# Turning batch 1's dilated q and k by DMA instead of on TensorE, and a new order at the start of an output stage

## The chip, the cores and the metric

The kernel runs on one core of one Trainium2 chip. The core has five engines with instruction queues of their own: TensorE (PE in the profile; its weight loads are PEld), VectorE (DVE), ScalarE (ACT), GpSimd (POOL) and SyncE (SP, which here only issues transfers). Sixteen DMA engines move data between the chip's memory and the core's on-chip memory (SBUF); TensorE writes its results to PSUM, eight banks of 128 x 512 float32. Each engine takes its instructions strictly in program order, so one that waits holds up all that stand behind it. The metric is the device time in microseconds (us).

## The reference: what is computed

Attention with two kinds of masks, then a gated feed-forward block on its result. Cut to what matters:

```python
batch, n_heads, seq, head_dim = (8, 8, 576, 64)          # q, k, v, float32
scores = scale * np.matmul(q, k.transpose(0, 1, 3, 2))
mask_plain = (rel >= 0) & (rel < 32)                     # heads 0-3
mask_dil = (rel >= 0) & (rel < 128) & (rel % 4 == 0)     # heads 4-7
attn = softmax over the positions that the mask leaves
x = (attn @ v), heads side by side                       # 4608 tokens x 512
g, val = x @ w_gate, x @ w_val                           # 512 x 1536 each
out = (gelu(g) * val) @ w_out                            # 1536 x 512
```

A dilated head sees only keys that are a multiple of four positions away, so its 576 positions fall into four classes of 144 that never meet. In scores and values the kernel handles a class as 128 + 16 positions.

## The kernel before: the parts that matter here

The 4,608 tokens are nine chunks of 512, c = 0 to 8. A chunk has a first feed-forward part (`ffn1`, twelve blocks `nb` of gate and value products with GELU) and an output stage (`ffn2`, four blocks `tb` of 128 tokens, each a chain of twelve matmuls over `u_all` and `wo`). The attention of the batches whose tokens come next is woven into the output stages. A batch has four units of work, two plain pairs of heads and two dilated ones; n = 4 to 7 are those of batch 1 (4 and 5 plain, 6 and 7 dilated). For each unit: scores on TensorE (`emit_s`, `s_of`), an exponential on ScalarE, a multiplication by the mask on VectorE (`mask_next`), the sums of the rows on TensorE (`den`), their reciprocals on VectorE (a 32x32 transpose, a reciprocal, a transpose back), the weighted values on TensorE (`num`) and a multiplication on VectorE that writes `xT`.

Scores need q and k with the head dimension on the partitions, so they must be transposed. For the dilated heads of batches 0 and 1 TensorE does this, from a tile that holds eight positions of a head per partition (72 partitions):

```python
    def load_eights(b):
        q8 = ldp.tile([R8, 2, HK, 8, D], F16, tag="qd", name=f"qd{b}")     # R8 = 72
        for t, src in ((0, q), (1, k)):
            tiles["last"] = nc.gpsimd.dma_start(
                out=q8[:, t].rearrange("p h r d -> p h (r d)"), in_=eights(src, b, HK, H)
            )
        return q8

    def t_dil(b, hp, q8, b0, engs):
        qtd_ = tiles["qT", b][1]
        for t in range(2):
            for hl in range(2):
                for r in range(4):
                    ...
                    nc.tensor.transpose(ps16[:, b0 + t, c0 : c0 + R8], ..., ident[0:R8, 0:R8])
            copy(engs[t], qtd_[:, t, 2 * hp : 2 * hp + 2]..., ps16[:, b0 + t, 0:S]...)
```

Batches 2 to 7 load four positions per partition, 128 partitions and a rest of 16, and let the DMA engines transpose. Transfers issued from GpSimd turn float32 into float16 on the way:

```python
    def load_qk_dil(b):
        qd = ldp.tile([P, 2, HK, 4, D], F16, tag="qd", name=f"qd{b}")
        rd = ldp.tile([16, 2, HK, 4, D], F16, tag="rd", name=f"rd{b}")
        for t, src in ((0, q), (1, k)):
            nc.gpsimd.dma_start(out=fl(qd[:, t]), in_=quads(src, b, HK, 0, 4 * P))
        for t, src in ((0, q), (1, k)):
            nc.gpsimd.dma_start(out=fl(rd[:, t]), in_=quads(src, b, HK, 4 * P, S))
        return qd, rd
```

`last_keys` copies the last 64 columns of every key class from `qTd` to `kTr`, which the dilated scores read as well:

```python
    def last_keys(b, h0, h1, eng=nc.vector):
        _, qtd_, ktr = tiles["qT", b]
        eng.tensor_copy(ktr[:, h0:h1], qtd_[:, 1, h0:h1, :, NCL - 64 : NCL])
```

The loads of batch 1, in program order (a `gate` makes a transfer wait until another one has landed):

```python
    load_w(2)                                   # POOL: wg, wv
    gate["dma"] = w1
    st1 = ldp.tile([R6, 2, HK, 6 * D], F32, tag="st", name="st1")
    for t, src in ((0, q), (1, k)):
        gated(nc.sync.dma_start(out=st1[:, t], in_=sixes(src, 1)))      # SP: plain q, k
    sv1 = new_v(1)
    new_qt(1)
    qd1 = load_eights(1)                        # POOL: dilated q, k
    wo1 = [load_wo(i) for i in range(3)][1]     # POOL: wo0, wo1, wo2
    load_v_dil(1)                               # POOL: vd, vr, vr
    q61 = ldp.tile([R6, 2, 6, HK, D], F16, tag="qp", name="qp1")
    for hp in range(2):
        for t in range(2):
            cast_six("pool", q61, st1, t, hp)   # POOL: four casts to float16
    gate["dma"] = wo1
    v_plain(1, sv1, nc.sync)                    # SP: plain v
    v_cast(1, sv1)
    tiles["plain", 2] = load_batch_plain(2)
```

In blocks 10 and 11 of the first feed-forward part TensorE transposes the plain q and k that those casts made:

```python
            if c == 0 and nb > 9:
                t_plain(1, q61, nb - 10, (4, 2)[nb - 10], ("act", "dve"))
```

Then comes the output stage of chunk 0, in which `third(tb, i)` is four of the twelve matmuls of block `tb`, on bank `tb`:

```python
            s_of(4)
            t_dil(1, 0, qd1, 0, ("dve", "dve"))
            t_dil(1, 1, qd1, 2, ("act", "dve"))
            mask_next()
            last_keys(1, 0, HK)
            third(0, 0)
            s_of(5)
            third(1, 0)
            mask_next()
            den(4, 0)
            s_of(6)
            third(0, 1)
            mask_next()
            third(1, 1)
            den(5, 0)
            s_of(7)
            third(0, 2)
            mask_next()
            den(6, 0)
            third(1, 2)
            ffn2(c, 2, 0, {3: [lambda: num(4, 4)], 8: [lambda: den(7, 0)]})
            store(c, 2, 0, "act")
            ffn2(c, 3, 1, {2: [lambda: num(5, 6)]})
            store(c, 3, 1, "act")
            num(6, 2)
            num(7, 4)
            gelu_table()
```

Of the kernel before, what the change touches and what calls it, by code (L numbers as in the profile page):

```python
# [21 lines left out]
def kernel(  # L22
# [10 lines left out]
    nc = tc.nc  # L33
# [3 lines left out]
    P = 128  # L37
    NHP = H // 2
    HK = H // 2
    NCL = S // DIL  # L40
# [117 lines left out]
    tiles = {}  # L158
# [82 lines left out]
    def load_eights(b):  # L241
        q8 = ldp.tile([R8, 2, HK, 8, D], F16, tag="qd", name=f"qd{b}")
# [5 lines that stand above are left out]
# [5 lines left out]
    def load_v_dil_rest(b):  # L253
        for m in range(2):
# [2 lines left out]
                in_=quads(v, b, HK, S - 256, S)[:, :, 2 * m * D : 2 * m * D + 2 * D],  # L257
            )

    def load_batch_plain(b):  # L260
        st = load_qk_plain(b)
        sv = new_v(b)
        v_plain(b, sv, nc.sync)
        return st, sv
# [5 lines left out]
    def load_batch_rest(b):  # L270
        st, sv = tiles["plain", b]
        qd, rd = load_qk_dil(b)
        qp = cast_qk_plain(b, st)
        load_v_dil(b)
        v_cast(b, sv)
        new_qt(b)
        qtp_, qtd_, _ = tiles["qT", b]
        dst = qtd_.rearrange("p t h m i -> p (t h m) i")
        nc.sync.dma_start_transpose(out=dst[:, :, 0:P], in_=qd.rearrange("p t h r d -> p (t h r d)"))
        nc.sync.dma_start_transpose(out=dst[:, :, P:NCL], in_=rd.rearrange("p t h r d -> p (t h r d)"))  # L280
        dst = qtp_.rearrange("p t h c -> p (t h) c")
        for kb in range(5):
            n = min(P, S - kb * P)
            nc.sync.dma_start_transpose(
                out=dst[:, :, kb * P : kb * P + n], in_=qp[0:n, kb].rearrange("p t h d -> p (t h d)")
            )
        last_keys(b, 0, HK, nc.gpsimd)
# [17 lines left out]
    def cast_six(eng, q6, st, t, hp):  # L305

        h = slice(2 * hp, 2 * hp + 2)
        copy(eng, q6[:, t, :, h, :], st[:, t, h, :].rearrange("p h (r d) -> p r h d", r=6))
# [305 lines left out]
    def ffn2(c, tb, bank, hooks=None, fcs=range(NNB)):  # L614
        for fc in fcs:
            for hook in (hooks or {}).get(fc, ()):
                hook()
            nc.tensor.matmul(  # L618
                ps[:, bank, :],
                u_all[:, fc, tb * P : (tb + 1) * P],  # L620
                wo_t[fc // 4][:, fc % 4, :],
                start=(fc == 0),
                stop=(fc == NNB - 1),
            )
# [69 lines left out]
    def den(n, b0, dt=None):  # L694
        emit_pv(n, b0, ("den",), wide=True)
        return norm_r(n, b0, wide=True, dt=dt)

    def num(n, b0):
        emit_pv(n, b0, ("num",))
        norm_x(n, b0)  # L700
# [35 lines left out]
        gated(nc.sync.dma_start(out=st1[:, t], in_=sixes(src, 1)))  # L736
    sv1 = new_v(1)
    new_qt(1)
    qd1 = load_eights(1)
    wo1 = [load_wo(i) for i in range(3)][1]  # L740
    load_v_dil(1)
    q61 = ldp.tile([R6, 2, 6, HK, D], F16, tag="qp", name="qp1")
    for hp in range(2):
        for t in range(2):
            cast_six("pool", q61, st1, t, hp)
    gate["dma"] = wo1
    v_plain(1, sv1, nc.sync)
    v_cast(1, sv1)
# [21 lines left out]
    for c in range(NCH):  # L770
        if 1 <= c and c + 2 < B:
            tiles["plain", c + 2] = load_batch_plain(c + 2)
            load_batch_rest(c + 2)
        pv_at = values_a.get(c, {})
        s_list = list(scores.get(c, ()))
        if c < 2:
            pairs = ((2, 3), (0, 1))
        else:
            pairs = (ends, (mm0 + 1, mm0 + 2))
        SB = 4 - mm0  # L780

        masks = []
        pend = None
        for nb in range(NNB):
            if nb == 0 and c < 2:
                ffn1_two(c, ((4, 5), (6, 7)) if c == 0 else ((6, 7), (0, 1)), range(NKC), False)
            elif nb == 0 and late:
                ffn1_two(c, pairs, (2, 3, 0, 1) if c in (2, 3) else range(NKC), True)
            elif nb > 1 or not (c < 2 or late):
                ffn1(c, nb, pairs[nb % 2])  # L790
            if pend is not None:
                (norm_both_x if is_plain(pend) else norm_x)(pend, SB)
                pend = None
            if nb in pv_at:
                pend = pv_at[nb]
                if is_plain(pend):
                    emit_both(pend, SB)
                    norm_both_r(pend, SB)
                else:
                    emit_pv(pend, SB, wide=True)  # L800
                    norm_r(pend, SB, wide=True)
            if c == 0 and nb > 9:
                t_plain(1, q61, nb - 10, (4, 2)[nb - 10], ("act", "dve"))
            if nb == NNB - 1 and c > 0 and s_list:
                n = s_list.pop(0)
                masks.append(emit_s(n, SB, pe_mask=n in biased))

        def s_next():
            if s_list:
                n = s_list.pop(0)  # L810
                masks.append(emit_s(n, SB, pe_mask=n in biased))

        def mask_next():
            mask = masks.pop(0) if masks else None
            if mask is not None:
                mask()


        if c == 0:
            load_batch_rest(2)  # L820

            def third(tb, i):
                ffn2(c, tb, tb, fcs=range(4 * i, 4 * i + 4))
                if i == 2:
                    store(c, tb, tb, "act")

            def s_of(n):
                masks.append(emit_s(n, 4))


            s_of(4)
            t_dil(1, 0, qd1, 0, ("dve", "dve"))
            t_dil(1, 1, qd1, 2, ("act", "dve"))
            mask_next()
            last_keys(1, 0, HK)
            third(0, 0)
            s_of(5)
            third(1, 0)
            mask_next()
            den(4, 0)  # L840
            s_of(6)
            third(0, 1)
            mask_next()
            third(1, 1)
            den(5, 0)
            s_of(7)
            third(0, 2)
            mask_next()
            den(6, 0)
            third(1, 2)  # L850
            ffn2(c, 2, 0, {3: [lambda: num(4, 4)], 8: [lambda: den(7, 0)]})
            store(c, 2, 0, "act")
            ffn2(c, 3, 1, {2: [lambda: num(5, 6)]})
            store(c, 3, 1, "act")
# [3 lines that stand above are left out]
        else:  # L858
            todo = list(values_b.get(c, ()))
            lone = c in values_b  # L860

            ends = (3, 0) if c == 1 else ends
            going = []

            def do(kind, tb):
                if kind == "s":
                    s_next()
                elif kind == "m":
                    mask_next()
                elif kind == "x":  # L870
                    norm_x(*going.pop(0))
                elif kind == "v":
                    n, flip = todo.pop(0), ends[tb % 2] != mm0
                    bank = mm0 + 1 - flip
                    emit_pv(n, bank, flip=flip)
                    norm_r(n, bank, flip=flip)
                    going.append((n, bank, flip))
                else:
                    n = todo.pop(0)
                    emit_pv(n, SB)  # L880
                    norm_parts(n, SB, min(S, (c + 2) * CH - n // NHP * S))

            for tb in range(4):
                at = [(fc, kind) for t, fc, kind in places.get(c, ()) if t == tb]
                hooks = {}
                for fc, kind in at:
                    if fc < NNB:
                        hooks.setdefault(fc, []).append(lambda kind=kind, tb=tb: do(kind, tb))
                bank = ends[tb % 2] if lone else mm0 + tb
                if c == NCH - 1 and tb == 3:  # L890
                    last_block(c, tb, bank)
                    break
                ffn2(c, tb, bank, hooks)
                store(c, tb, bank, "dve" if c > 5 and tb == 3 else "act")
                for fc, kind in at:
                    if fc == NNB:
                        do(kind, tb)
            if lone:
                gelu_table()

            late = lone and len(values_b[c]) > 2
            if c == 3:
                mm0 = 4 - mm0
            if c == 3 or not lone:
                ends = (mm0, mm0 + 3)
            while masks:
                mask_next()
# [28 lines left out]
```

The softmax here doesn't subtract the row's maximum and nothing guards it: scores larger than these inputs give would overflow.

## Time and profile before

| | |
|---|---|
| time, median of 3 runs | 348.75 us (348.43 to 348.92) |
| span of the profiled execution | 347.0 us |
| TensorE busy | 336.0 us, 97% of the span |
| VectorE busy | 201.8 us |
| ScalarE busy | 148.2 us |
| GpSimd busy | 84.0 us |
| matmuls of `ffn1`, mean | 379 ns each, pipelined |
| VectorE transpose of 128 x 576 float32 | about 0.78 us |

A line of the timeline or of a group gives the start or the count, the length, the engine, the source line, the operation and, in brackets, how long the engine had been idle and what released it. In the chain of waits each line is a start, a length and what ran, followed back from the last instruction to what released each step. The "us to landing" of a transfer counts from its issue to its completion. "SPq" is the queue of SyncE in which it issues transfers. TensorE's matmuls overlap, and their ends are modelled, so sums of its busy times are longer than the time they take.

### The profile page before, as it was taken

To read this page: it belongs to the slowest core of one execution; us is meant where nothing else is said; L and a number is where in the kernel's file an instruction comes from. 1 tells how busy PE (TensorE), PEld (TensorE's weight loads), DVE (VectorE), ACT (ScalarE), POOL (GpSimd) and SP (SyncE) were. 2 spreads that over 40 slices of the span, in tenths; PEclk is the share of its full clock that TensorE was granted. 3 is DMA by queue.
4 is the path that set the end of the run, shared out by engine and by line. 5 is a ranking of instruction groups with operands and counts; after the bars stand their busy time and mean duration, and the time that the engine had idled before them with its cause. 6 is when DMAs were issued, how large, how long until landed. Compare 5 with 4: busy or idle time off the path is not lost.

```text
span 347.0 us, 6006 instructions
## 1 busy us (share of the span) xinstructions
PE 336.0 (97%) x2342; PEld 163.7 (47%) x2342; DVE 201.8 (58%) x309; ACT 148.2 (43%) x220; POOL 84.0 (24%) x123
## 2 busy tenths in 40 slices
PE   8879999999999999999999999999999999999996
PEld 3644454444544445444544454444444444444443
DVE  3784488443794359674878576975498423303320
ACT  1753473535543447336553547336633223223321
POOL 8893304630630540351006300510000000000000
PEclk9999999999999999999999999999999999999999
DMA  8999999999999999898169925991100020020002
GB/s 179 225 201 223 205 200 192 184 147 258 178 107 256 191 152 171 201 162 121 62 159 168 157 73 137 195 126 55 70 0 0 32 91 1 2 91 30 2 30 91
DMA packets 107516, 44.44 MB, mean 128 GB/s; under 512 B 83328, under 2 KB 102912, under 8 KB 107488
## 3 DMA queue, kind: packets, MB, share of 16 engines
q1 hardware_dynamic: 84192, 31.01, 39.2%
q0 software_dynamic: 22752, 12.33, 28.9%
q10 hardware_dynamic: 544, 0.72, 0.8%
q8 instruction: 18, 0.29, 0.4%
q14 instruction: 10, 0.08, 0.1%
HBM read 39.85 MB, written 9.44 MB: 142 GB/s over the span
## 4 chain that ended last, share of the span: by engine, by line
PE 70%; DVE 13%; DMA 10%; issue 3%; ACT 2%; SPq 1%; POOL 1%; DVEq 0%; POOLq 0%; ACTq 0%
PE ps L584 42%; PE ps L618 21%; PE ps L472 4%; DMA st<-in_k_dram 4%; DMA sv<-in_v_dram 3%; DMA wv<-in_moe_w_val_dram 3%; DVE dt L500 2%; DVE dt L533 2%; DVE u_all L607 2%; DVE xT L559 2%; DVE rb L544 2%; DVE P L400 2%; DVE xT L510 1%; PE ps L390 1%; DVE rc L542 1%
## 5 line engine op out<-in xcount | busy, mean ns | idle before, releaser
L607 DVE SCALAR_TENSOR_TENSOR u_all<-g,ps 128x512 f16<-128x512 f16 x108 | 72.8, 684 | 76.7 <-PE ps L584 67.9
L606 ACT ACTIVATE g<-ps 128x512 f16<-128x512 f32 x108 | 63.9, 596 | 123.3 <-PE ps L584 122.8
L584 PE MATMUL ps<-xT,wg 128*128 128x512 f16 x432 | 114.0, 379 | 1.2 <-POOL xT L707 0.7
L584 PE MATMUL ps<-xT,wv 128*128 128x512 f16 x432 | 113.8, 379 | 0.2 <-DVE u_all L607 0.2
L618 PE MATMUL ps<-wo,u_all 128*128 128x512 f16 x420 | 96.9, 380 | 0.2 <-DVE qTd L303 0.2
L584 PEld LDWEIGHTS <-wv 128*128 128x128 f16 x432 | 42.2, 98 | 52.8 <-issue 2.9
L584 PEld LDWEIGHTS <-wg 128*128 128x128 f16 x432 | 41.3, 98 | 48.9 <-issue 1.1
L618 PEld LDWEIGHTS <-u_all 128*128 128x128 f16 x420 | 38.4, 98 | 44.7 <-issue 0.8
L629 ACT ACTIVATE osb<-ps 128x512 f32<-128x512 f32 x33 | 19.7, 597 | 38.8 <-PE ps L618 37.8
L228 POOL CAST qp<-st 128x2048 f16<-128x2048 f32 x6 | 11.4, 1893 | 97.8 <-DMA st<-in_k_dram 64.8
L544 DVE STREAM_TRANSPOSE rb<-rc 128x576 f32<-128x576 f32 (+4 forms) x34 | 25.3, 743 | 1.3
L533 DVE STREAM_TRANSPOSE dt<-ps 128x576 f32<-128x576 f32 x21 | 16.3, 778 | 12.4 <-PE ps L472 12.3
L392 ACT ACTIVATE P<-ps 128x1152 f16<-128x1152 f32 x16 | 18.1, 1130 | 11.8 <-PE ps L390 11.8
L370 ACT ACTIVATE P<-ps 128x960 f16<-128x960 f32 x16 | 15.5, 970 | 11.0 <-PE ps L360 11.0
L559 DVE TENSOR_TENSOR xT<-ps,rb 128x576 f16<-128x576 f32 x16 | 17.9, 1129 | 2.2 <-PE ps L472 1.9
L400 DVE TENSOR_TENSOR P<-P,mask_d 128x1152 f16<-128x1152 f16 x13 | 9.8, 751 | 9.7 <-ACT P L392 9.7
L400 DVE TENSOR_TENSOR P<-P,mask_p 128x1344 f16<-128x1344 f16 x14 | 11.8, 856 | 2.9 <-ACT P L371 2.9
L472 PE MATMUL ps<-P,ones 128*64 128x96 f16 (+5 forms) x174 | 11.3, 244 | 2.1 <-DVE P L400 1.5
L472 PEld LDWEIGHTS <-ones 128*64 128x64 f16 x174 | 7.2, 109 | 11.5 <-issue 8.6
L631 DVE TENSOR_SCALAR osb<-ps 128x512 f32<-128x512 f32 x2 | 1.4, 691 | 18.2 <-PE ps L618 18.2
L255 POOL DMA_DIRECT2D vr<-in_v_dram x16 | 9.9, 632 | 5.3 <-DMA wv<-in_moe_w_val_dram 3.6
L500 DVE STREAM_TRANSPOSE dt<-ps 64x576 f32<-64x576 f32 x14 | 10.9, 781 | 0.4
(88 smaller groups left out, 247.8 us busy)
## 6 DMA issues: line engine op xcount, KB each, us to landing
out_dram<-osb SPq DMA_DIRECT2D x35, 256.0 KB, 2.0
sv<-in_v_dram SPq DMA_DIRECT2D x40, 128.0 KB, 3.3
st<-in_q_dram SPq DMA_DIRECT2D x24, 128.0 KB, 3.1
st<-in_k_dram SPq DMA_DIRECT2D x24, 128.0 KB, 3.1
vd<-in_v_dram POOLq DMA_DIRECT2D x7, 256.0 KB, 6.5
wo<-in_moe_w_out_dram POOLq DMA_DIRECT2D x3, 512.0 KB, 19.7
qd<-in_q_dram POOLq DMA_DIRECT2D x6, 256.0 KB, 5.4
qd<-in_k_dram POOLq DMA_DIRECT2D x6, 256.0 KB, 6.9
```

Of the source, the lines that this page charges most:

```text
L392: nc.scalar.activation(pt, ps[:, b0 : b0 + 4, 0:DW], AF.Exp, bias=0.0, scale=scale)
L400: nc.vector.tensor_tensor(pt, pt, mb, ALU.mult)
L472: nc.tensor.matmul(o, lhs, rhs, start=st, stop=True, skip_group_check=True)
L500: nc.vector.transpose(dt[64 * hl : 64 * hl + 64].rearrange("p b c -> p (b c)"), both_rows(1 - hl, b0, hl))
L533: nc.vector.transpose(dst, den)
L544: nc.vector.transpose(rb[:, 0 : 32 * nb].rearrange("p (b c) -> p b c", c=32), bass.AP(tensor=rc.tensor, offset=rc.offset, ap=[rc.ap[0], [1 ...
L559: nc.vector.tensor_tensor(dst.rearrange("p (i m s) -> p i m s", m=2, s=2), num, rb.rearrange("p (s m i) -> p i m s", s=2, m=2), ALU.mult,)
L584: nc.tensor.matmul(ps[:, bank, :], w[:, kc, ns], xT[kc][:, tok], start=first, stop=end)
L606: nc.scalar.activation(g, ps[:, banks[0], :], AF.Gelu)
L607: nc.vector.scalar_tensor_tensor(u_all[:, nb, :], g, USCALE, ps[:, banks[1], :], ALU.mult, ALU.mult)
L618: nc.tensor.matmul(ps[:, bank, :], u_all[:, fc, tb * P : (tb + 1) * P], wo_t[fc // 4][:, fc % 4, :], start=(fc == 0), stop=(fc == NNB - 1),)
L629: nc.scalar.activation(osb, ps[:, bank, :], AF.Copy, bias=0.0, scale=1.0 / USCALE)
```

## The change: what it does and what it is for

Batch 1's dilated q and k are loaded as batches 2 to 7 load theirs (four positions per partition and a rest), and two DMA transposes, issued from SyncE before the loads of plain v, write `qTd`. That takes 32 transposes off TensorE and four copies out of PSUM off VectorE and ScalarE. The output stage of chunk 0 no longer has `t_dil`; in its place it begins with three thirds of output blocks, so that TensorE has work while the first exponential runs. `last_keys` moves behind the second mask, and the places of `num(4)` and `den(7)` in block 2 move from before matmuls 3 and 8 to before 5 and 9.

```diff
+    def turn_dil(b, qd, rd):
+        dst = tiles["qT", b][1].rearrange("p t h m i -> p (t h m) i")
+        nc.sync.dma_start_transpose(out=dst[:, :, 0:P], in_=qd.rearrange("p t h r d -> p (t h r d)"))
+        nc.sync.dma_start_transpose(out=dst[:, :, P:NCL], in_=rd.rearrange("p t h r d -> p (t h r d)"))
... (load_batch_rest uses turn_dil for the same two transposes as before)
     new_qt(1)
-    qd1 = load_eights(1)
+    qd1, rd1 = load_qk_dil(1)
     wo1 = [load_wo(i) for i in range(3)][1]
     load_v_dil(1)
     q61 = ldp.tile([R6, 2, 6, HK, D], F16, tag="qp", name="qp1")
     for hp in range(2):
         for t in range(2):
             cast_six("pool", q61, st1, t, hp)
+    turn_dil(1, qd1, rd1)
     gate["dma"] = wo1
     v_plain(1, sv1, nc.sync)
...
             s_of(4)
-            t_dil(1, 0, qd1, 0, ("dve", "dve"))
-            t_dil(1, 1, qd1, 2, ("act", "dve"))
+            third(0, 0)
+            third(1, 0)
+            third(0, 1)
+            mask_next()
+            s_of(5)
+            den(4, 0)
+            third(1, 1)
+            third(0, 2)
             mask_next()
             last_keys(1, 0, HK)
-            third(0, 0)
-            s_of(5)
-            third(1, 0)
+            s_of(6)
+            den(5, 0)
+            third(1, 2)
             mask_next()
-            den(4, 0)
-            s_of(6)
-            third(0, 1)
+            s_of(7)
+            den(6, 0)
             mask_next()
-            third(1, 1)
-            den(5, 0)
-            s_of(7)
-            third(0, 2)
-            mask_next()
-            den(6, 0)
-            third(1, 2)
-            ffn2(c, 2, 0, {3: [lambda: num(4, 4)], 8: [lambda: den(7, 0)]})
+            ffn2(c, 2, 0, {5: [lambda: num(4, 4)], 9: [lambda: den(7, 0)]})
             store(c, 2, 0, "act")
```

More of the change, by code (lines that the diff above doesn't have):

```diff
@@ L276, in load_batch_rest @@
         new_qt(b)
[L277 to L281, printed above, removed]
+        turn_dil(b, qd, rd)
+        dst = tiles["qT", b][0].rearrange("p t h c -> p (t h) c")
         for kb in range(5):
```

## The prediction, made before the result was known

> **What bounds the kernel now.** I read the page's busy times first, then the chain of waits, then the timeline around the change: GpSimd and SyncE from 22 us, all engines from 40 to 62 us. TensorE sets the time almost everywhere, so a microsecond that it gains or idles in the output stage of chunk 0 should reach the end.
>
> ```profile
> PE 336.0 (97%) x2342; PEld 163.7 (47%) x2342; DVE 201.8 (58%) x309; ACT 148.2 (43%) x220; POOL 84.0 (24%) x123
> ```
>
> The chain of waits (start, length, what ran) runs through the change's neighbourhood like this:
>
> ```profile
> 27.55 13.09 DMA st<-in_k_dram
> ...
> 40.69 0.83 POOL qp L301
> ...
> 41.57 0.43 PE ps L314 x6
> 42.00 1.73 PE ps L584 x8
> 43.73 0.27 PE ps L314 x6
> ...
> 49.23 0.86 DVE P L400
> 50.08 0.70 DVE dt L533
> ...
> 51.18 0.78 DVE rb L544
> 51.96 0.64 DVE P L400
> ...
> 62.13 20.83 PE ps L584 x96
> ```
>
> Two things are to be seen. The landing of batch 1's plain k and GpSimd's cast of it release TensorE at 41.57: that cast has no slack. And from 49 to 53 us the chain is VectorE's, masks and reciprocals.
>
> GpSimd's part of the timeline (start, length, then the idle time before it and its releaser):
>
> ```profile
> 23.73 0.77 POOL L244 DMA_DIRECT2D qd<-in_q_dram  x1
> 24.47 0.74 POOL L244 DMA_DIRECT2D qd<-in_k_dram  x1
> 25.18 2.31 POOL L154 DMA_DIRECT2D wo<-in_moe_w_out_dram  x3
> 27.43 0.80 POOL L250 DMA_DIRECT2D vd<-in_v_dram  x1
> 29.93 0.63 POOL L255 DMA_DIRECT2D vr<-in_v_dram  x1 [1.70 <-DMA wg<-in_moe_w_gate_dram]
> 34.20 0.61 POOL L255 DMA_DIRECT2D vr<-in_v_dram  x1 [3.65 <-DMA wv<-in_moe_w_val_dram]
> 36.29 0.82 POOL L301 CAST qp<-st 96x768 f16<-96x768 f32 x1 [1.48 <-DMA st<-in_q_dram]
> 40.69 2.36 POOL L301 CAST qp<-st 96x768 f16<-96x768 f32 x3 [3.58 <-DMA st<-in_k_dram]
> ```
>
> Here each vr load waits for a weight load with which it shares no data, and each time it is the load issued eight before it on GpSimd (wg and wv of the last third). [...] The casts stand behind those waits.
>
> The pieces that the change removes, from the timeline of all engines:
>
> ```profile
> 44.57 1.50 PE L332 MATMUL ps<-ident,qd 72*128 72x72 f16 x32
> 45.52 2.08 DVE L303 COPY qTd<-ps 128x576 f16<-128x576 f16 x3
> 46.32 1.02 PE L618 MATMUL ps<-wo,u_all 128*128 128x512 f16 x4 [0.24 <-DVE qTd L303]
> 47.21 0.65 ACT L299 COPY qTd<-ps 128x576 f16<-128x576 f16 x1
> ```
>
> After that TensorE is nearly gapless until 62.06, because every wait for VectorE has a third of a block in front of it.
>
> [...] The 1.70 and 3.65 us above agree: GpSimd itself stood. [...] The packet records agree: from 34 to 36 us, 163 packets of 1,024 bytes from GpSimd's queue and 166 of 1,536 from SyncE's, about one for one. [...]
>
> **The change part by part.**
>
> Step 1, what TensorE saves: 1.50 us for the 32 transposes and 0.24 us of waiting for the copies, 1.7 us in all, on TensorE's path. VectorE loses 2.08 us of copies.
>
> Step 2, the casts come later. The dilated loads are now four (q, k, rest of q, rest of k) where there were two. So every later load moves two places in the round of eight. In the order of instructions the two vr loads no longer wait for wg and wv but for dilated q and dilated k. Before, those were issued at 23.73 and 24.47 and took 15.0 and 16.6 us to land (narrow windows of the transfers): 38.7 and 41.1. The bytes are the same, in halves of the packet size: the records give 367 packets of 512 bytes per us alone (188 GB/s) against 202 of 1,024 (207 GB/s), so 1,152 small ones cost 3.1 us where 576 cost 2.85, and the rests, a ninth, come after q and k. I keep 41.0 for k. Then the second vr issues for 0.6 us, the first cast (q) runs 41.7 to 42.5, the second (k) to 43.4. TensorE used k at 41.57 and now at 43.4: 1.8 us lost. [...]
>
> Step 3, the new order against VectorE. I laid out the stage with the durations above, without step 2's shift. `s_of(4)` 44.2; three thirds at 0.86 us to 47.2; exponential 4 ends at 47.3 as before (its table load sets that); `s_of(5)` to 47.85; mask 4 to 48.36. Now `den(4)` stands directly behind, with no third between: TensorE idles 0.5 us. VectorE then does transpose, reciprocal, transpose (1.95 us), mask 5 (0.86) and `last_keys` (0.3), ending at 51.95. `s_of(6)` needs that, while TensorE has finished its two thirds at 50.55: 1.4 us idle. The reciprocals of 5 and mask 6 end at 55.65, while TensorE has reached `den(6)` at 54.3: 1.35 us idle. `num(4)` comes at 57.2 against 55.33, with two fewer matmuls (0.43 us) left after it. Sum: +0.5 +1.4 +1.35, minus 1.7 of step 1, gives +1.5 us. So the order alone loses what the removal brings, and more: before, masks stood ahead of the reciprocals on VectorE, and thirds filled the waits.
>
> Step 4, the landing of the transposes. SyncE can issue them from 41.1 (2.75 and 1.15 us of issue, the 62.87 and 65.73 entries of batch 2), and their first packets follow 1.8 us later, at about 43. GpSimd's queue then still holds 76 of 96 wo packets per DMA engine, then vd and vr. A transpose of this size is 2,048 packets of 256 bytes, 128 per DMA engine, about 20 ns each alone. One for one with wo's 79 ns, 76 of them take 7.5 us (to 50.5); with the rest of the queue they end at about 53. The rest's transpose landed 3 us after the first in batch 2. So `qTd` is complete at 53 to 56. With step 2's shift `last_keys` would come at 53.5, so it stalls for 0 to 2.5 us: I take 1.0. Plain v, behind the transposes on SyncE, lands at about 58 and is cast by 59.5, just before the delayed `num(4)`.
>
> Sum: 1.8 + 1.5 + 1.0 = +4.3 us. Later loads move with the stage: batch 2's transposes ended about 5 us before their first use at 82.9, and that margin hardly changes. 348.75 + 4.3 = 353.05, rounded to 353.0.
>
> **The rivals.** Rival one: the transposes on TensorE were the cost and everything else is hidden, -1.7 us, 347.0. The nearly full TensorE row speaks for it; against it, VectorE's pieces in the chain and the lost fillers. It also needs the casts to be on time. Rival two: the casts are late but the new order packs well (1.8 - 1.7): no difference, 348.8. Rival three: the transposes starve behind the weights until 57 or later and v follows them: +7 us or more, 356. For it, rest transposes landing up to 8.2 us after issue in a busy stretch; against it, GpSimd's queue empties by about 54 and at 20 ns a packet little is then left.
>
> **Range and chances.** Step 2 is the surest (the waits are in the order of instructions; 0.8 to 2.2 us by when k lands). Step 3 rests on known durations, within 0.7 us. Step 4 is the loosest, 0 to 3.5 us. Low: 0.8 + 0.8 - 0.2 makes 350.0 with rounding down; high: 2.2 + 2.2 + 2.6 makes 355.8. Over 2% slower is above 355.7, which needs nearly all of step 4's upper end: 0.10. Faster by 2% is out of reach of a 1.7 us saving: 0.01.
>
> **What would show it.** Step 2: the second vr load's wait names dilated k, the first cast starts at about 41.7, and TensorE idles before L316 by some 1.8 us. Step 3: idle TensorE before `den(4)`, `s_of(6)` and `den(6)`, released by VectorE. Step 4: VectorE's `last_keys` released by a DMA of `qTd` at 53 us or later; if it is ready by 51 the one-for-one sharing is wrong. The second feed-forward part should start near 66.4 instead of 62.06. If it starts before 62, the prediction is wrong in steps 2 or 3; if the later stages change, in the margin of the loads.

## The result and the profile after

| | before | after |
|---|---|---|
| time, median (range, executions) | 348.59 us (348.35 to 348.92, 4) | 353.06 us (352.28 to 355.25, 4) |
| span of the profiled execution | 347.0 us | 351.0 us |
| first matmul of the second `ffn1` | 62.06 us | 65.73 us |
| from there to the end of the span | 284.9 us | 285.3 us |

The ratio is 1.0138, with a 95% interval of [1.0091, 1.0185]: the change makes the kernel 4.5 us slower. In the two profiles the difference is 4.0 us, and all but 0.3 us of it is lost before 65.73 us, in the stage that the change touches. First the busy times from the page after:

```profile
PE 336.5 (96%) x2310; PEld 163.1 (46%) x2310; DVE 200.4 (57%) x306; ACT 147.9 (42%) x219; POOL 85.8 (24%) x125
```

TensorE has 32 instructions fewer, and its busy time is no shorter. The chain of waits after (start, length, what ran) tells what came in their place:

```profile
24.25 14.87 DMA qd<-in_k_dram
...
39.18 6.44 SPq L262
...
45.74 7.81 DMA qTd<-rd
...
53.65 0.30 DVE kTr L273
...
54.00 0.44 PE ps L392 x8
54.43 0.72 PE ps L474 x6
...
55.17 0.80 DVE dt L535
...
65.80 20.83 PE ps L586 x96
```

Before, this stretch of the chain ran through plain k, GpSimd's cast, TensorE and VectorE. Now it is the load of dilated k, the issue of its transpose (6.44 us in SyncE's queue) and the landing of the rest's transpose, 24.25 to 53.6 us without a piece of arithmetic. The row after the transposes is `last_keys`.

GpSimd's timeline after (start, length, idle time before it and releaser) answers to the one of before:

```profile
24.98 0.57 POOL L238 DMA_DIRECT2D rd<-in_q_dram  x1
25.50 0.57 POOL L238 DMA_DIRECT2D rd<-in_k_dram  x1
...
33.76 0.74 POOL L250 DMA_DIRECT2D vd<-in_v_dram  x1 [3.04 <-DMA wv<-in_moe_w_val_dram]
38.29 0.62 POOL L255 DMA_DIRECT2D vr<-in_v_dram  x1 [3.79 <-DMA qd<-in_q_dram]
39.40 0.61 POOL L255 DMA_DIRECT2D vr<-in_v_dram  x1 [0.49 <-DMA qd<-in_k_dram]
40.01 3.13 POOL L303 CAST qp<-st 96x768 f16<-96x768 f32 x4
```

The two vr loads wait for dilated q (3.79 us) and dilated k (0.49 us), each the load issued eight before it on GpSimd, as the prediction said; vd's wait of 3.04 us is for wv, again eight before. Why it is the eighth is not shown. The casts come behind these loads in the program: the first begins at 40.01 us, as the issue of the second vr ends (39.40 + 0.61). But k landed at 39.15 us, not at 41.0, and the four casts end at 43.1 us; before they ended at 43.05.

The timeline of all engines after, where TensorE stands still:

```profile
41.67 0.43 PE L316 MATMUL ps<-ident,qp 96*128 96x96 f16 x6 [0.33 <-POOL qp L303]
...
48.37 0.48 PE L474 MATMUL ps<-P,ones 128*64 128x512 f16 x6 [0.45 <-DVE P L402]
...
53.06 0.29 PE L392 MATMUL ps<-qTd 64*128 64x128 f16 x4 [2.39 <-DMA qTd<-qd]
...
53.65 0.29 DVE L273 COPY kTr<-qTd 128x512 f16<-128x512 f16 x1 [2.06 <-DMA qTd<-rd]
...
54.00 0.19 PE L392 MATMUL ps<-qTd,kTr 64*128 64x32 f16 x2 [0.65 <-DVE kTr L273]
...
55.07 1.89 PE L620 MATMUL ps<-wo,u_all 128*128 128x512 f16 x4
...
57.77 0.44 PE L474 MATMUL ps<-P,ones 128*64 128x288 f16 x4 [0.21 <-DVE P L402]
```

L316 is within 0.1 us of where it was (41.57), so the casts cost next to nothing. The gap is at the first dilated scores: 2.39 us for the large transpose, then 0.65 us for VectorE's copy, which waited for the small one. And then something that nobody had forecast: four matmuls of L620 take 1.89 us, where four of the same line and shape take 1.04 later in the same stage. A table by stretches of time (stretch, its length, busy time of each engine, granted TensorE clock, DMA share, GB/s) shows why:

```profile
50.00:52.00 2.00, 0.68 (x4) 0.10 (x1) 1.52 (x2) 0.60 (x1) 0.00 (x0) 1.00 1.52 82
52.00:53.00 1.00, 0.00 (x0) 0.00 (x0) 0.00 (x0) 0.00 (x0) 0.00 (x0) 1.00 1.25 226
...
54.00:55.00 1.00, 1.00 (x14) 0.61 (x14) 0.00 (x0) 0.53 (x1) 0.00 (x0) 0.54 1.35 218
55.00:56.00 1.00, 1.00 (x8) 0.39 (x4) 0.79 (x2) 0.60 (x1) 0.00 (x0) 0.50 1.36 218
...
58.00:59.00 1.00, 1.00 (x8) 0.41 (x5) 0.76 (x1) 0.72 (x1) 1.00 (x2) 1.00 1.37 223
```

After the gap the clock is at half (0.50) until about 57.5 us. This also goes into the busy time of TensorE, as slower matmuls count as busy: the same 2,310 instructions at full clock come to 335.5 us in e4 below, against 336.5 here and 336.0 for the 2,342 before.

### The profile page after: what moved, and what is told of

The parts are those of the page before. It is cut to its first block, busy times and chain, and to the rows that moved or that the text cites. A ratio compares the mean times of both kernels' runs of the same rounds, so it can differ in the third digit from the quotient of the medians.

```text
span 351.0 us, 5943 instructions
## 1 busy us (share of the span) xinstructions
PE 336.5 (96%) x2310; PEld 163.1 (46%) x2310; DVE 200.4 (57%) x306; ACT 147.9 (42%) x219; POOL 85.8 (24%) x125
## 3 DMA queue, kind: packets, MB, share of 16 engines
q1 hardware_dynamic: 86320, 31.60, 43.1%
## 4 chain that ended last, share of the span: by engine, by line
PE 68%; DVE 13%; DMA 10%; SPq 3%; POOL 3%; issue 3%; ACT 0%; DVEq 0%; POOLq 0%; ACTq 0%
PE ps L586 41%; PE ps L620 20%; DMA qd<-in_k_dram 4%; PE ps L474 4%; DMA sv<-in_v_dram 3%; DMA qTd<-rd 2%; SPq L262 2%; DVE rb L546 2%; DVE dt L535 2%; DVE dt L502 2%; DVE u_all L609 2%; DVE xT L561 2%; DVE P L402 1%; DVE xT L512 1%; PE ps L392 1%
## 5 line engine op out<-in xcount | busy, mean ns | idle before, releaser
L620 PE MATMUL ps<-wo,u_all 128*128 128x512 f16 x420 | 97.5, 382 | 0.0
L620 PEld LDWEIGHTS <-u_all 128*128 128x128 f16 x420 | 38.6, 98 | 44.9 <-issue 1.0
L631 ACT ACTIVATE osb<-ps 128x512 f32<-128x512 f32 x33 | 19.7, 598 | 41.1 <-PE ps L620 41.0
L212 POOL CAST vp<-sv 128x1024 f16<-128x1024 f32 x8 | 8.5, 1066 | 14.2 <-DMA sv<-in_v_dram 14.2
L273 POOL COPY kTr<-qTd 128x512 f16<-128x512 f16 (+1 forms) x7 | 4.5, 645 | 27.5 <-DMA qTd<-rd 18.6
```

Source lines behind the costliest of these rows:

```text
L620: nc.tensor.matmul(ps[:, bank, :], u_all[:, fc, tb * P : (tb + 1) * P], wo_t[fc // 4][:, fc % 4, :], start=(fc == 0), stop=(fc == NNB - 1),)
L631: nc.scalar.activation(osb, ps[:, bank, :], AF.Copy, bias=0.0, scale=1.0 / USCALE)
```

## The experiments

Each time has its own runs of the kernel before on the same chip; their medians were 348.56, 348.62, 348.59 and 348.78 us in the four sets. The measure used below beside the time is the length of the stage in the profile, from the start of mask 4 on VectorE to the first matmul of the second `ffn1`: 47.51 to 62.06, 14.55 us, in the kernel before, and 47.45 to 65.73, 18.28 us, after.

### Order without transposes, and transposes without order (e1, e4, e5)

The change has three parts: other loads, DMA transposes, another order. The first kernel keeps the loads and the new order and drops the transposes; `qTd` of batch 1 is zero from the start, so this leaves the dilated scores' data out of the computation and keeps all their work. The second has the old order as well (without `t_dil`). The third is the whole computation of the change, in the old order.

```diff
# e1
     new_qt(0)
+    new_qt(1)
+    nc.vector.memset(tiles["qT", 1][1], 0.0)
...
-    new_qt(1)
     qd1, rd1 = load_qk_dil(1)
...
-    turn_dil(1, qd1, rd1)
# e4: e1, and the output stage of chunk 0 as before, without its two t_dil lines
# e5: the change, and the output stage of chunk 0 as before, without its two t_dil lines
```

Order without transposes (e1):

> The changed kernel without its two DMA transposes: batch 1's qTd is a constant set at the start (its dilated scores are left out of the computation), the four loads of dilated q and k and the new order stay. Theory A (the transposes land late, behind the weights, and that wait is the loss): TensorE's gap before the first dilated scores shrinks from 3.0 us, the stage starts on time, and if the new order packs as it should the time is 348.6 - 1.7 = 346.9. Theory B (step 3 of the prediction: the new order alone loses 1.5 us on VectorE): about 350.1, with 1.4 us of idle TensorE before those scores and 1.3 before den(6).

Neither (e4):

> As the run without transposes, but with the old order of the stage less its t_dil: the most that taking the transposes off TensorE can bring in the old order. Both theories: 1.7 us under before, 346.9. If step 3 is right the new order stands 3.2 us above this; if the new order packs well they are equal within 0.5.

Transposes in the old order (e5):

> The changed kernel with the old order of the stage (without t_dil): the DMA transposes alone. If they land at 53 to 53.5 as in the changed kernel, VectorE stands at the copy of the last keys from 48.2 to 53.5 with mask 5 behind it, and everything after it is 5.3 us later than in the old order with a constant qTd (348.9): 354 to 355.5, and the new order is worth 1 to 2 us beside late transposes. If the new order costs its 1.35 us in any case: 351.7.

| | time | ratio to before | stage |
|---|---|---|---|
| e4: new loads, free transposes, old order | 348.88 us (12 executions) | 1.0008 [0.9997, 1.0018] | 14.71 us |
| e1: new loads, free transposes, new order | 349.90 us (15) | 1.0050 [1.0029, 1.0071] | 16.58 us |
| after: with DMA transposes, new order | 353.06 us (4) | 1.0138 [1.0091, 1.0185] | 18.28 us |
| e5: with DMA transposes, old order | 354.66 us (4) | 1.0176 [1.0152, 1.0199] | 20.46 us |

e4 is the surprise of this set. It has no transposes at all, on TensorE or by DMA, and gains nothing: its second `ffn1` starts at 62.06 us as before. The timeline of e4 shows where the 1.5 us of `t_dil` went:

```profile
44.68 1.28 ACT L372 ACT_TABLE_LOAD   x1
45.97 0.97 ACT L372 ACTIVATE P<-ps 128x960 f16<-128x960 f32 x1
46.84 0.48 ACT L373 ACTIVATE P<-ps 128x384 f16<-128x384 f32 x1
46.99 0.23 PE L362 MATMUL ps<-qTp 64*128 64x160 f16 x1 [1.39 <-ACT P L372]
...
47.37 0.45 PE L362 MATMUL ps<-qTp 64*128 64x160 f16 x9 [0.16 <-ACT P L373]
```

`s_of(5)` waits for exponential 4, which waits for ScalarE's table load; the 32 transposes had filled exactly that wait, and without them TensorE idles 1.39 + 0.16 us in the same place. They were free.

From e4 to e1 is the price of the order alone: 1.0 us. From e1 to after is the price of the transposes: 3.2 us. With them the new order is 1.6 us better than the old one (e5), but it does not follow that it hides the delay. The timeline of e5:

```profile
51.59 0.39 PE L392 MATMUL ps<-qTd 64*128 64x128 f16 x4 [2.64 <-DMA qTd<-qd]
...
52.88 3.60 PE L620 MATMUL ps<-wo,u_all 128*128 128x512 f16 x8
```

Those eight matmuls take 1.90 us in e4. The clock is at 0.50 from 51.25 to 58.08 us in e5, twice as long as in the change. From its scores with `kTr` (52.50 us) to the second `ffn1` TensorE waits for nothing and takes 15.05 us; in e4, in the same order at full clock, this takes 12.75 (49.31 to 62.06). So some 2.3 us of e5 are the clock's, more than the 1.6 us by which the new order is ahead. That the new order is better beside late transposes is not shown.

The timeline of e1 shows its waits:

```profile
48.69 0.48 PE L474 MATMUL ps<-P,ones 128*64 128x512 f16 x6 [0.45 <-DVE P L402]
...
51.46 1.36 POOL L212 CAST vp<-sv 128x1024 f16<-128x1024 f32 x1 [7.99 <-DMA sv<-in_v_dram]
51.84 1.13 DVE L273 COPY kTr<-qTd 128x512 f16<-128x512 f16 x1
...
53.02 0.19 PE L392 MATMUL ps<-qTd,kTr 64*128 64x32 f16 x2 [1.80 <-DVE kTr L273]
...
56.39 0.44 PE L474 MATMUL ps<-P,ones 128*64 128x288 f16 x4 [1.29 <-DVE P L402]
```

The three waits are at `den(4)`, `s_of(6)` and `den(6)`, the places that step 3 named. One is longer than the arithmetic: `last_keys` took 1.13 us instead of 0.29, beside GpSimd's cast of v. The profiled execution is one of the longer ones of e1 (352.26 us), so its lengths, and the stage in the table, are not those of the median.

### Why dilated k landed early (e2, e3)

Step 2 failed on a landing: 39.15 us instead of 41.0. Is it the size of the packets (the pieces in which the DMA engines move a transfer), or the form of the old load with its 72 partitions? Both kernels are e1 with another load of dilated q and k. One uses the load of before (72 partitions, 1,024-byte packets), one a load of nine positions per partition (64 partitions, 1,152-byte packets, no rest).

```diff
# e2
-    qd1, rd1 = load_qk_dil(1)
+    qd1 = load_eights(1)
# e3
+    def load_nines(b):
+        q9 = ldp.tile([64, 2, HK, 9, D], F16, tag="qd", name=f"qn{b}")
+        for t, src in ((0, q), (1, k)):
+            ...  out=q9[:, t]..., in_=src[b, HK:H].rearrange("h (p r) d -> p h (r d)", r=9)
-    qd1, rd1 = load_qk_dil(1)
+    qd1 = load_nines(1)
```

> As the run without transposes, but dilated q and k are loaded as before, eight positions on 72 partitions in two transfers, and not used. For why step 2 failed (dilated k landed at 39.15 instead of 41.0, plain k at 38.3 instead of 40.65). If the form of the load is the cause: dilated k lands near 41 and plain k near 40.6, as before. If something else in the changed kernel is the cause, they land near 39.2 and 38.3.

> As the run before it, with nine positions on 64 partitions (packets of 1,152 bytes, larger than the 1,024 of before). If the number of partitions is the cause [...]: dilated k lands near 39 and plain k near 38.5. If the size of the packets is the cause: 41 or later, and plain k at 40.6 or later.

One execution each: 349.83 and 349.44 us. Issue and landing of dilated k and of the plain k that shares the DMA engines with it:

| | packets of dilated k | issued | us to landing | landed | plain k landed (issue about 27.5) |
|---|---|---|---|---|---|
| e2 (as before): 72 partitions | 1,024 bytes | 24.16 | 17.3 | 41.5 | 40.6 |
| e3: 64 partitions | 1,152 bytes | 24.13 | 15.2 | 39.3 | 40.2 |
| after: 128 partitions and 16 | 512 bytes | 24.25 | 14.9 | 39.15 | 38.3 |

e3 has the largest packets and lands with the small ones. So the 2.2 us belong to the form with 72 partitions, not to the packets (the kernel before, with the same form, has 41.1). The 128 partitions carry 256 KB of the 288 KB, as the rest is a transfer of its own. Plain k, which shares the engines with these loads, lands 2 us earlier beside the packets of 512 bytes (38.3) than beside the two larger sizes (40.6 and 40.2); between those two the order is the reverse, so packet size as its cause is not shown. The forecast had taken the old landing of k over into the new form; that was the mistake. Why the form with 72 partitions lands later is not shown.

Both kernels also show the order without the collision of e1: TensorE waits 0.45, 0.95 and 1.29 us in e3, with `last_keys` at 0.28 us, and the stage is 15.74 us in e2 and in e3, 1.03 longer than in e4. That is the 1.0 us of the times.

### What made the transposes late, and what the gap costs (e6, e7, e8)

Three kernels, each with the change's order. The first fills the gap with ten matmuls whose result nobody reads. The second leaves out the loads of wo1 and wo2 (constants in their place), so that GpSimd's queue holds 1 MB less ahead of the transposes. The third does the whole computation and only moves the loads of dilated v behind the landing of the transposes.

```diff
# e6
             last_keys(1, 0, HK)
+            warm(10, 4)
             s_of(6)
# e7
-    wo1 = [load_wo(i) for i in range(3)][1]
+    wo1 = load_wo(0)
# e8
-    load_v_dil(1)
...
-    turn_dil(1, qd1, rd1)
+    gate["dma"] = turn_dil(1, qd1, rd1)     # the rest's transpose
+    load_v_dil(1)                           # its first load waits for the gate
```

> The changed kernel with ten matmuls of 512 columns on constants, their result unused, in TensorE's gap before the first dilated scores (50.7 to 52.9). If the halved TensorE clock after the gap (0.5 from 54 to 57.5) costs time: the clock stays at 1.0, the four matmuls of third(1, 2) take 1.04 us instead of 1.89, and the time falls by 0.7 to 1.3 us, to about 352. If VectorE's chain hides it: 353, unchanged.

> The changed kernel with two of three parts of w_out set to a constant at the start instead of loaded (the products with them are left out of the true computation). If the weights in GpSimd's queue are what delays the transposes: SyncE issues the first in about 2.8 us instead of 6.4, both land by 47, the gap before the dilated scores falls to that of the run without transposes, and the time is that run's, 349.5 to 350.5. If the transposes are slow by themselves: they land after 49 and the time stays above 351.

> The changed kernel, whole computation, with the three loads of dilated v moved behind the transposes (they wait for the second to land, and stand behind the four casts on GpSimd). If packets alternate one for one, the transposes have the DMA engines to themselves once w_out is in (about 47) and land near 49.5: the gap shrinks to that of the run without transposes and the time is 349.9 to 350.7. If dilated v is not what they wait for: landing at 52 or later, 352.5 to 353.

| | issue of the large transpose | its us to landing | landed (large, rest) | time | ratio to before |
|---|---|---|---|---|---|
| after | 6.44 us | 13.8 | 53.0, 53.5 | 353.06 us | 1.0138 [1.0091, 1.0185] |
| e6: gap filled | 6.43 us | | 52.7, 53.2 | 352.70 us | 1.0114 [1.0099, 1.0129] |
| e8: loads of v held | 5.46 us | 11.9 | 50.9, 51.4 | 351.03 us | 1.0074 [1.0048, 1.0099] |
| e7: 1 MB of weights less | 4.14 us | 7.2 | 46.25, 48.0 | 350.40 us | 1.0043 [1.0029, 1.0058] |

SyncE's part of the timeline of e7, its queue rows being the issues:

```profile
39.05 4.14 SPq L262 DMA_TRANSPOSE qTd<-qd  x1
43.31 1.15 SPq L263 DMA_TRANSPOSE qTd<-rd  x1
```

The transposes are slow because GpSimd's queue is full: take two of the three weights away and the large one lands in 7.2 us instead of 13.8. They land before they are needed, and e7 is then within 0.5 us of e1, which has none. (It also has earlier casts, as GpSimd waits less: the first starts at 34.35 us instead of 40.01, and mask 4 at 46.46 us. And as in e1 the cast of v meets `last_keys`, which takes 1.13 us, so that TensorE waits 1.80.) Even the issue is shorter (4.14 us instead of 6.44). Holding 384 KB of dilated v back (e8) brings 2.1 us of landing and 2.0 us of time. (Here too the casts come earlier, no longer standing behind the vr loads: the first starts at 34.31 us, and mask 4 at 46.42, 1.0 before that of the change.) Its landing is later than the 49.5 us expected from one-for-one sharing. The records of packets show where: 2,027 of the 2,048 packets of the large transpose begin by 48.85 us, the last 21 only up to 50.1, and it counts as landed at 50.9. Why the last ones come late stays open.

e6 separates the gap from the clock. Its clock is 1.00 all through, and four matmuls take 1.04 us again, but the timeline shows the next wait in the place of the slow matmuls:

```profile
52.73 0.29 PE L392 MATMUL ps<-qTd 64*128 64x128 f16 x4 [0.15 <-DMA qTd<-qd]
...
53.66 0.19 PE L392 MATMUL ps<-qTd,kTr 64*128 64x32 f16 x2 [0.65 <-DVE kTr L273]
...
57.39 0.44 PE L474 MATMUL ps<-P,ones 128*64 128x288 f16 x4 [1.66 <-DVE P L402]
```

VectorE's chain of masks and reciprocals, begun late, bounds what follows, and so a slow TensorE mostly takes up slack. From the scores with `kTr` to the second `ffn1` it is 11.73 us in the profile of the change (54.00 to 65.73), 11.70 in e6 and 11.34 in e3, which has neither the gap nor the half clock. (In e6 one mask, begun during the cast of v, takes 1.08 us instead of 0.72, and so the wait of 1.66 us is longer than e3's 1.29.) The half clock costs the profiled execution some 0.4 us, an estimate from 11.73 and 11.34. The median falls by 0.4 us too, which four executions of each do not separate from nothing. What the fill takes away is the spread: e6's four executions lie between 352.57 and 352.98 us, those of the change between 352.28 (mean clock 0.994) and 355.25 (0.988).

A longer stretch at half clock is not hidden. The profiled executions of e7 and e8 are the longest of each (352.24 and 352.69 us). In them the clock is at 0.50 from 53.38 to 60.21 and from 53.12 to 59.94 us, and the same stretch, with the same instructions, takes 13.57 us in both, against 11.34 in e3. So their landings can be compared, but their stages (18.82 and 19.03 us) hold some 2 us of the clock's.

### A version that gives it back (e11, e12, e13)

With the transposes landing at 51.4 us an order can be looked for that fits them: `den(5)` and its reciprocals first, `third`s before each wait, `s_of(7)` and `den(6)` inside block 2, `num(4)` after it. e11 is e8 in that order. e12 is e11 with unit 6's mask added by TensorE as a bias instead of multiplied by VectorE.

```diff
# e11: e8, and
             third(1, 1)
-            third(0, 2)
             mask_next()
+            third(0, 2)
+            third(1, 2)
             last_keys(1, 0, HK)
-            s_of(6)
             den(5, 0)
-            third(1, 2)
-            mask_next()
-            s_of(7)
-            den(6, 0)
+            s_of(6)
             mask_next()
-            ffn2(c, 2, 0, {5: [lambda: num(4, 4)], 9: [lambda: den(7, 0)]})
+            ffn2(c, 2, 0, {5: [lambda: s_of(7)], 9: [lambda: den(6, 0), mask_next]})
             store(c, 2, 0, "act")
-            ffn2(c, 3, 1, {2: [lambda: num(5, 6)]})
+            num(4, 4)
+            ffn2(c, 3, 1, {6: [lambda: den(7, 0)], 8: [lambda: num(5, 6)]})
# e12: e11, and
-                masks.append(emit_s(n, 4))
+                masks.append(emit_s(n, 4, pe_mask=n == 6))
```

> Whole computation: dilated v held behind the transposes, and an order made for a qTd that lands at 51.4: sums and reciprocals of 4, mask 5 and all six thirds before the copy of the last keys, the sums of 5 ahead of the first dilated scores, the scores of 7 and sums of 6 inside block 2, the weighted values of 4 after it. If VectorE's order is what made the new stage slow (its masks and reciprocals are 12.8 us from the first mask), TensorE starts the next first part at about 61.4 against 62.06 before and the time is 347.6 to 348.4, under before. If the landing still rules: 349.5 or more.

> The same, with the mask of unit 6 as a bias that TensorE adds (0.66 us of matmuls) instead of 0.72 us of VectorE. If VectorE bounds the stage: 0.3 to 0.6 us under the run without the bias. If TensorE bounds it by then: equal or up to 0.6 us over.

e11 took 349.35 us, 1.0021 [1.0011, 1.0031]; e12 350.20 us, 1.0047 [1.0034, 1.0061] (four executions; a fifth, of 357.74 us at a mean clock of 0.948, is left out). The bias makes it 0.9 us worse, a little more than the 0.66 us of matmuls that it adds. In e11's stage TensorE waits only 0.45 us before `den(4)` and 0.44 before the scores with `kTr`, so there was hardly any slack for them. e11's miss is more telling. Its stage is 14.40 us and its second `ffn1` starts at 61.08 us, 1.0 earlier than before. But the long run of matmuls in the third, which begins at 102.95 us in the chain of before, begins at 103.35: the gain is lost again in the output stage of chunk 1, which neither the change nor e11 touches. VectorE's two plain masks there, in the kernel before:

```profile
95.17 1.66 DVE L400 TENSOR_TENSOR P<-P,mask_p 128x1344 f16<-128x1344 f16 x2
```

and in e11, with GpSimd and TensorE beside them:

```profile
94.19 3.22 DVE L402 TENSOR_TENSOR P<-P,mask_p 128x1344 f16<-128x1344 f16 x2
...
94.22 1.25 POOL L255 DMA_DIRECT2D vr<-in_v_dram  x2
95.43 1.27 POOL L212 CAST vp<-sv 128x1024 f16<-128x1024 f32 x1
...
95.86 0.49 PE L474 MATMUL ps<-P,ones 128*64 128x64 f16 x10 [0.99 <-DVE P L402]
...
96.65 1.02 POOL L216 CAST vt<-sv 128x256 f16<-128x256 f32 x1
```

The two masks take twice as long (3.22 us against 1.66) while GpSimd issues batch 3's loads and casts. In the kernel before GpSimd had ended the same work by 93.3 us. Those loads and casts had moved 3.6 us back (the cast of vp from 91.83 to 95.43), the masks 1.0 us forward, and they met. To test this, e13 changes the order of GpSimd's work for batch 3 and nothing else:

```diff
# e13: e11, and in load_batch_rest
-        load_v_dil(b)
-        v_cast(b, sv)
+        if b != 3:
+            load_v_dil(b)
+            v_cast(b, sv)
...      (the two transposes, last_keys)
+        if b == 3:
+            load_v_dil(b)
+            v_cast(b, sv)
```

> e11 with one thing changed: batch 3's load of dilated v and its cast of v stand behind the cast of its last keys on GpSimd, so that they come later than the two plain masks of batch 2 that took 3.22 us together in e11 (1.66 us before). If the overlap of GpSimd's work with those masks is what gave e11's 1.1 us back: the two masks take about 1.7 us again, the wait for them on TensorE (0.99 us) falls to 0.2 or less, and the time is 347.6 to 348.2 us, under the kernel before. Rival: the masks are late because the loads behind them are (the wait only changes its name): 349.3 as e11, or more if the later cast of v now comes too late for batch 3's values.

The timeline of e13:

```profile
94.26 1.65 DVE L406 TENSOR_TENSOR P<-P,mask_p 128x1344 f16<-128x1344 f16 x2
...
95.16 0.49 PE L478 MATMUL ps<-P,ones 128*64 128x64 f16 x10 [0.21 <-DVE P L406]
...
97.12 0.76 POOL L250 DMA_DIRECT2D vd<-in_v_dram  x1
97.88 1.24 POOL L255 DMA_DIRECT2D vr<-in_v_dram  x2
99.09 1.07 POOL L212 CAST vp<-sv 128x1024 f16<-128x1024 f32 x1
100.07 0.43 POOL L216 CAST vt<-sv 128x256 f16<-128x256 f32 x1
```

The masks are back at 1.65 us for the two, the casts at 1.07 and 0.43, and the wait on TensorE at 0.21. The third `ffn1` starts at 102.00 us, 0.95 earlier than before. The rival, that late loads would hold the masks back whatever runs beside them, falls. The time is 348.38 us (22 executions), against 348.78 for the kernel before in the same set (27): 0.9987 [0.9981, 0.9994], some 0.2 us above the upper end of what was expected. In the profiles the last `ffn1` starts 0.95 us earlier than before (311.65 against 312.60) and the span is 0.6 us shorter (346.4 against 347.0), so not all of it reaches the time; where the rest goes was not followed. e13 does the whole computation, and it is the only version here with DMA transposes that beats the kernel before, by an eighth of a per cent.

## Why the prediction was right in its sum and wrong in its terms

The prediction was 353.0 us, in a range of 350.0 to 355.8; the measurement is 353.06. It went by a sum of 1.8 + 1.5 + 1.0 us, where the 1.5 held a saving of 1.7 inside. The runs give the same total from other terms:

| term | predicted | measured | by |
|---|---|---|---|
| steps 1 and 2: TensorE's saving, late casts | -1.7 and +1.8 | +0.3 together, within the noise | e4 against before |
| step 3: waits for VectorE in the new order | +3.25 | +1.0 | e1 against e4 |
| steps 1 and 3 as the prediction summed them | +1.5 | +1.3 | e1 against before |
| step 4: waiting for the transposes | +1.0 | +3.2 | after against e1 |

That the sum agrees to 0.1 us is in part luck: step 2's 1.8 us did not come, and step 4 came 2.2 us larger. In part it is not, because the landing set the end either way (step 4 below). In the profile after, the second `ffn1` starts at 65.73 us, where 66.4 was forecast.

- **Step 1, "What TensorE saves: 1.7 us"**: did not come. The durations were right, the place was not asked about: `t_dil` stood in a wait for the table load and exponential 4. The prediction had even used that exponential's end (47.3 us) as a bound in step 3, without asking what the removed transposes had been doing until then.
- **Step 2, "the casts come later"**: the waits were right to the name of the releaser (dilated q for 3.79 us, dilated k for 0.49), the size was not. The term mis-sized is "I keep 41.0 for k": it landed at 39.15, because the new form lands sooner than the old one (the change against e2, 39.15 and 41.5). The casts then end where they had, and L316 comes 0.1 us later, not 1.8.
- **Step 3, the order against VectorE**: the three waits are where it put them, and nearly as long: 0.5, 1.4 and 1.35 us forecast, 0.45, 0.95 and 1.29 in e3. What was wrong is to count all of them as loss and then set step 1's 1.7 against it. The old order without `t_dil` has a wait of its own of 1.55 us (e4), so the order as such costs 1.0 us. Steps 1 and 3 taken together, as it summed them, were nearly right.
- **Step 4, the landing of the transposes**: 53.0 and 53.5 us, at the early end of the "53 to 56" that one-for-one sharing gave. The sharing is seen in the packet records: from 44 to 50 us 1,226 packets of GpSimd's queue and 1,243 of SyncE's. The issue was not as forecast: from 39.18 instead of 41.1, and 6.44 us instead of 2.75; the first packets came at 43.1 all the same. The term mis-sized is the stall, "I take 1.0". It was counted from a `last_keys` that step 2's lateness had already pushed to 53.5. Without that lateness VectorE stood ready at 51.6 and waited 2.06 us, and TensorE waited 2.39 + 0.65. Landing is a point in time: what delays the work before it shortens the stall, and steps 2 and 4 could not both be paid in full. The halved clock, which no step had, may have added to it: some 0.4 us, not clear of the spread.
- **"That margin hardly changes"** (later loads): held for the change itself, whose later stages have the old length (285.3 us to the end against 284.9). It does not hold in general, as e11 shows: there loads and casts that came 3.6 us later cost over 1 us, not by arriving late but by what they ran into.
- **The rivals**: one (hidden transposes, -1.7) falls with e4. Two (late casts, order packs well) falls with the casts, which were not late, and with e1, whose order costs 1.0 us over e4's. Three (starving until 57) falls with the landing at 53.5; its cause, the full queue ahead, is what e7 and e8 confirmed (7.2 and 11.9 us to landing instead of 13.8).

## What to carry to other kernels

Before counting what a removed instruction saves, look at what its engine would wait for in its place: the 1.50 us of transposes ran inside a wait, and taking them away only showed it (1.39 + 0.16 us in e4). A transfer that is to take over an engine's work must be asked when it lands: the same transpose took 13.8 us here behind the full queue of GpSimd, 11.9 with 384 KB less in it and 7.2 with 1 MB less. A wait that ends at a fixed landing gets shorter by whatever delays the work before it, so the two are not added.

## What the runs showed of the hardware that was not expected

- **The clock after a gap.** TensorE's granted clock went to half (0.50) for 3.41 us in the profile after (54.08 to 57.49), behind 3.41 us in which TensorE was busy for 0.38. In e5 it was at half for 6.83 us (51.25 to 58.08), and in the profiled executions of e7 and e8 for 6.83 and 6.82, there after single waits of only 1.80 us (e7) and 1.31 and 0.64 us (e8). In the 3.41 us just before, TensorE was busy for 1.10 us in e5, 1.52 in e8 and 1.67 in e7. e1 has the same wait of 1.80 us, and its clock stayed at 1.00. So the length of a wait alone does not tell whether the clock falls; what does is not shown.
- **VectorE beside GpSimd.** A 128x512 copy took 1.13 us instead of 0.29, and each 128x1344 mask 1.65 us on average instead of 0.87, beside GpSimd's casts and issues of loads. The second mask of e11, begun during a cast, took 1.68 us. Which one is held up varies: in the change the mask at 57.00 us began 0.03 us before the cast of vt and took its usual 0.72 us, and the cast 0.95 instead of 0.40. The first mask of e11 took 1.62 us although the cast began 1.24 us after it; only issues of loads ran beside it until then, and beside those another mask of e11 (57.19 us) took 0.72. What held it up is not shown.
- **The form of a load, not the size of its packets.** 72 partitions of 1,024-byte packets landed in 17.3 us and 64 partitions of 1,152 bytes in 15.2, 288 KB each, in the same queue (one execution each). 128 partitions of 512 bytes took 14.9 us, for 256 KB.
- **The issue of a DMA transpose beside other transfers.** It took 2.75 us in batch 2 of the kernel before, where all 2,181 packets that ran meanwhile were SyncE's own, and 6.44 us in the change, beside 1,220 packets of GpSimd's queue. With less in that queue it took 5.46 us (e8) and 4.14 (e7).
